# Summing the rotation's two products with accumulating transfers instead of vector adds, in a fused attention and feed-forward kernel

## The chip, the core and the metric

One core of a Trainium2 chip runs the whole program. The metric is the device time of one execution in microseconds, taken here as the median of three executions. TensorE (PE in the rows, with its weight loads shown apart as PEld), VectorE (DVE), ScalarE (ACT), GpSimd (POOL) and SyncE (SP) each work through their own list of instructions in order; transfers run on 16 DMA engines beside them.

## The reference

Four sequences, eight heads, 576 positions, 64 columns a head. Queries and keys are first rotated, then attention runs, and its output goes through two feed-forward blocks.

```python
def rotate(x):
    x1, x2 = (x[..., :half], x[..., half:])
    return np.concatenate([x1 * cos - x2 * sin, x1 * sin + x2 * cos], axis=-1)
q_rot, k_rot = (rotate(q), rotate(k))
scores = scale * np.matmul(q_rot, k_rot.transpose(0, 1, 3, 2))
attn = softmax(scores)            # minus the row's maximum, exp, over the row's sum
attn_out = np.matmul(attn, v)
...
x = x_attn.reshape(2304, 512)
x = ((x @ w1) * (x @ w2)) @ w3 @ w_out                       # first block
out = np.maximum(np.maximum(x @ u1, x @ u2), x @ u3) @ u_out # second block
```

All arrays are float32 on the host's side.

## The kernel before

Every float32 number that enters a matmul is split into a high part and a low part, which three matmuls multiply (high by high, low by high, high by low). Two heads make a pair, with their 64 columns on 128 partitions, so attention is 16 pairs, numbered p = 0 to 15.

For each pair, `prepare(p)` makes the rotated keys (e = 1) and queries (e = 0). The host lays each operand out twice, once as it is and once with its halves swapped, so the rotation is: load both copies (tile `qk`, two planes of 128 x 576; for pair 1 the tile is called `early`), multiply plane 0 by the cosine table and plane 1 by the signed sine table (line 612), and **sum the two planes into plane 0** (line 614). ScalarE then casts the sum into the high part in `st` (line 618), and a subtraction makes the low part (line 619). `st` and a small tile `z` (the last 64 positions of both heads, line 441) are what the score matmuls read. There are two `st` buffers, so the parts of pair p can only be written when the scores of pair p - 2 are done. There is one `qk` buffer for keys and one for queries.

After that, per pair: scores on TensorE (tile `s`, line 423), the row's maximum on VectorE (line 668), exp on ScalarE (line 671, tile `p`), transposes on TensorE (tile `t`, line 676), their split on ScalarE and VectorE (lines 441 and 708, tile `pt`), the product with v (tile `pv`), and the scaling by the reciprocal row sums (`inverse`, lines 681 and 683, and `rows_done`). Between these, TensorE folds two weight matrices into one (tile `m` from `wo` and `w`), and then runs the first block's two products (also tile `m`). The weights arrive as 64-bit words that VectorE and ScalarE turn into float32 (`convert`, lines 506, 509 and 511). From 458 us on no attention work is left and TensorE runs the two blocks.

**What sets the order.** Each operation is a task with an engine, a priority and a planned duration. A planner in the program walks the tasks in planned time and puts each ready task of the lowest priority next on its engine. A table of numbers, `MOVES`, perturbs the priorities, and also the engine of those tasks that can run on one of two engines (`either`). So the table fixes each engine's list, and it is a part of the program text. A transfer's task has a `tail`, the planned length of the transfer after its issue. Loads and stores are all issued by SyncE (`load`, line 444).

Of the kernel before, what the change touches and what calls it, by code (L numbers as in the profile page):

```python
# [46 lines left out]
    10000024, 10000032, 10000048, 10000067, 10000110, 10000112, 10000169, 10000173, 10000183, 10000227, 10000237,  # L47
    10000252, 10000323, 10000357, 10000392, 10000453, 10000476, 10000488, 10000538, 10000610, 10000693, 10000728,
    10000735, 10000773, 10000840, 10000846, 10000909, 10001099, 10001126, 10001173, 10001205, 10001233, 10001384,
    10001401, 10001457, 10001485, 10001511, 10001518, 10001545, 10001635, 10001784, 10001833, 10001865, 10001872,  # L50
    10001929, 10002157, 10002158, 10002193, 10002284, 10002338, 10002497, 10002607, 10002618, 10002634, 10002684,
    10002970, 10003189, 10003196, 10003281, 10003343, 10003405, 10003407, 10003435, 10003527, 10003634, 10003636,
    10003647, 10003666, 10003686, 10003773, 10004011, 10004536, 10004770, 10004918, 10004919, 10004999, 10005035,
    10005145, 10005476, 10005486, 10005506, 10005662, 10005664, 10005765, 10005914, 10006123, 10006241, 10006294,
    10006442, 10006576, 10007147, 10007203, 10007507, 10007547, 10007556, 10007604, 10007777, 10007815, 10008037,
    10008371, 10008436, 10008857, 10009245, 10009375, 10009463, 10009964, 10010205, 10010668, 10010822, 10011063,
    10011153, 10011320, 10011733, 10011754, 10012451, 10013224, 10013724, 10013750, 10013752, 10014503, 10014800,
    10015034, 10015238, 10015292, 10016008, 10016071, 10016400, 10016686, 10016975, 10016998, 10017598, 10018086,
    10018994, 10019298, 10019480, 10019796, 10019820, 10020198, 10020898, 10021153, 10021422, 10021641, 10021659,
    10022452, 10022683, 10022959, 10023141, 10023268, 10023299, 10023504, 10023897, 10024188, 10024325, 10024358,  # L60
    10024944, 10026610, 10027292, 10027429, 10027638, 10027768, 10028459, 10028793, 10030569, 10031137, 10031647,
    10031679, 10032588, 10033141, 10034705, 10034759, 10036016, 10036114, 10036487, 10037496, 10037920, 10038523,
    10038572, 10038623, 10038861, 10038948, 10039345, 10039953, 10040004, 10040208, 10041169, 10041777, 10042003,
    10042306, 10042544, 10043181, 10043748, 10043993, 10044060, 10044981, 10045250, 10046335, 10047230, 10048349,
    10050783, 10052317, 10053102, 10053375, 10053441, 10054365, 10054616, 10055368, 10055784, 10056263, 10056510,
    10058185, 10058223, 10058413, 10058664, 10060609, 10061682, 10061930, 10063544, 10063652, 10063701, 10064328,
    10064930, 10065410, 10065600, 10065736, 10065897, 10066392, 10068294, 10068310, 10069270, 10069399, 10069478,
    10070709, 10070855, 10071006, 10071578, 10071647, 10071991, 10072861, 10074691, 10075956, 10076571, 10076918,
    10077155, 10077393, 10077402, 10078340, 10079070, 10079133, 10080360, 10080621, 10081686, 10081820, 10082428,
    10083020, 10083021, 10083344, 10084928, 10085257, 10086848, 10087495, 10088943, 10089683, 10090879, 10091498,  # L70
    10091855, 10092674, 10092784, 10092916, 10093174, 10094606, 10094899, 10098752, 10101220, 10101843, 10101960,
    10102171, 10103117, 10105007, 10105660, 10107129, 10108351, 10109018, 10110088, 10113960, 10116148, 10116306,
    10116538, 10118489, 10119480, 10123241, 10124490, 10126498, 10126937, 10127867, 10128934, 10129888, 10132550,
    10134240, 10135241, 10136106, 10138483, 10139877, 10140809, 10141009, 10141359, 10141814, 10142075, 10142417,
    10142735, 10143382, 10143576, 10144461, 10145622, 10146303, 10147616, 10149250, 10149696, 10151815, 10151995,
    10153576, 10155729, 10157912, 10159162, 10159394, 10166681, 10169703, 10170189, 10171770, 10171897, 10173462,
    10176946, 10180597, 10181204, 10181835, 10182805, 10184517, 10186706, 10187211, 10188223, 10189780, 10193794,
    10194085, 10196598, 10197990, 10205021, 10205075, 10206304, 10207559, 10212827, 10213856, 10218775, 10234307,
    10235000, 10235644, 10238566, 10239970, 10266620, 10267709, 10275199, 10275926, 10279327, 10281026, 10283592,
    10287879, 10290827, 70012376, 70015660, 70026858, 70030643, 70045947, 70049814, 70051889, 70054017, 70055280,  # L80
    70056770, 70066295, 70067872, 70074298, 70078855, 70083392, 70083724, 70084529, 70086923, 70087171, 70087261,
# [1129 lines left out]
```

## Time and profile before

| | |
|---|---|
| median of three executions | 926.19 us (925.84 to 928.98) |
| profiled execution, own time | 927.38 us |
| its span, first to last instruction | 925.4 us |
| around the span | 1.98 us |
| TensorE busy | 891.0 us, 96% of the span |
| VectorE busy | 633.0 us, 68% |
| ScalarE busy | 475.9 us, 51% |
| GpSimd busy | 342.4 us, 37% |
| granted TensorE clock, mean | 0.998 of 2.4 GHz |

The profiled execution is 1.19 us above the median, so a change in the span is read against 925.4 us, and the forecast is then made on the median. A busy share is a mean over stages with different limits; the stages are read apart further down.

### The profile page before, as it was taken

Reading aid. Unit: us, or ns where it says so; the run is one execution under the profiler, and the core shown is the slowest. Engines: PE = TensorE matmul, PEld = TensorE weight load, DVE = VectorE, ACT = ScalarE, POOL = GpSimd, SP = SyncE. Lnnn points to the kernel's source line nnn. Section 1 sums busy time; section 2 is a strip of 40 time slices with the busy share of each in tenths; the row PEclk is TensorE's granted clock in tenths of the full one; section 3 lists DMA queues with packets and bytes.
Section 4 is the critical chain, followed back from the end, with each engine's and each line's share of the span. In section 5 each row is a group of like instructions: output and inputs, shape, how many; then the busy total and the mean of one; then the engine's idle time right before and its main releaser. Section 6 shows DMA issues by size and latency. Waiting matters only on the chain.

```text
span 925.4 us, 16273 instructions
## 1 busy us (share of the span) xinstructions
PE 891.0 (96%) x5922; PEld 823.8 (89%) x5922; DVE 633.0 (68%) x1133; ACT 475.9 (51%) x1054; POOL 342.4 (37%) x332
## 2 busy tenths in 40 slices
PE   1898999999999999999999999999999999999998
PEld 1666769989999999999998999999999999999886
DVE  6997988898867677687766333657988577578300
ACT  4677887876757577567544222434323322334411
POOL 3645767766436366522110000433332333232000
PEclk9999999999999999999999999999999999999999
DMA  8454546542333123310147543323324114255511
GB/s 265 134 188 153 165 154 209 149 142 84 100 103 97 44 92 93 97 50 18 37 153 213 199 127 89 103 86 97 98 86 140 55 46 148 68 163 195 201 57 68
DMA packets 80287, 110.31 MB, mean 119 GB/s; under 512 B 27984, under 2 KB 61008, under 8 KB 80208
## 3 DMA queue, kind: packets, MB, share of 16 engines
q1 hardware_dynamic: 80208, 109.29, 37.4%
q8 instruction: 46, 0.75, 0.3%
q14 instruction: 33, 0.27, 0.1%
HBM read 83.76 MB, written 25.50 MB: 118 GB/s over the span
## 4 chain that ended last, share of the span: by engine, by line
PE 80%; DVE 9%; DMA 7%; issue 2%; ACT 1%; SPq 1%; POOL 0%; DVEq 0%; ACTq 0%
PE q L423 46%; PE m L423 15%; PE t L676 7%; PE pv L423 6%; PE s L423 6%; DVE pt L708 3%; DMA raw<-in_w3t_dram 3%; DVE sm L668 2%; DMA raw<-in_w_dram 2%; DVE raw L509 1%; DMA rawc<-in_w3t_dram 1%; SPq L444 1%; DMA vr<-in_vv_dram 1%; DVE cw L511 1%; ACT pt L441 0%
## 5 line engine op out<-in xcount | busy, mean ns | idle before, releaser
L708 DVE TENSOR_TENSOR pt<-t,pt 128x320 fp32r<-128x320 f32 (+3 forms) x256 | 132.4, 528 | 34.5 <-ACT pt L441 29.4
L441 ACT CAST pt<-t 128x320 fp32r<-128x320 f32 (+3 forms) x234 | 103.5, 456 | 51.9 <-PE t L676 24.9
L423 PE MATMUL pv<-pt,v 128*128 128x256 f32 (+1 forms) x576 | 113.2, 317 | 5.1 <-DVE pt L708 4.0
L668 DVE TENSOR_REDUCE sm<-s 128x1 f32<-128x576 f32 x144 | 103.9, 749 | 19.8 <-PE s L423 18.8
L423 PE MATMUL q<-gt,wp 128*128 128x384 f32 x576 | 100.0, 334 | 0.0
L423 PEld LDWEIGHTS q<-gt,wp 128*128 128x128 f32 x576 | 99.8, 188 | 0.0
L423 PEld LDWEIGHTS pv<-pt,v 128*128 128x128 f32 x576 | 82.8, 189 | 15.7 <-DVE pt L708 9.5
L423 PE MATMUL s<-st 64*128 64x288 f32 x768 | 71.7, 316 | 18.7 <-ACT st L618 11.7
L423 PEld LDWEIGHTS s<-st 64*128 64x128 f32 x768 | 55.6, 190 | 32.5 <-ACT st L618 11.7
L423 PE MATMUL q<-yc__7620,u 128*128 128x384 f32 x378 | 71.2, 340 | 0.0
L423 PE MATMUL q<-yc__7946,u 128*128 128x384 f32 x378 | 70.8, 340 | 0.0
L423 PE MATMUL q<-yc__7376,u 128*128 128x384 f32 x378 | 70.5, 340 | 0.0
L423 PEld LDWEIGHTS q<-yc__7946,u 128*128 128x128 f32 x378 | 67.1, 188 | 0.1
L423 PEld LDWEIGHTS q<-yc__7620,u 128*128 128x128 f32 x378 | 67.1, 188 | 0.0
L423 PEld LDWEIGHTS q<-yc__7376,u 128*128 128x128 f32 x378 | 67.1, 188 | 0.0
L441 ACT COPY tmp<-q 128x384 f32<-128x384 f32 x45 | 21.5, 479 | 84.7 <-PE q L423 84.5
L441 ACT COPY ga<-q 128x512 f32<-128x512 f32 (+2 forms) x34 | 16.9, 497 | 65.6 <-PE q L423 61.6
L1066 POOL TENSOR_TENSOR tmp<-tmp 128x384 f32<-128x384 f32 x20 | 22.6, 1132 | 72.3 <-ACT tmp L441 72.3
L423 PE MATMUL q<-tail,tail 128*128 128x512 f32 x216 | 49.1, 389 | 0.0
L423 PEld LDWEIGHTS q<-tail,tail 128*128 128x128 f32 x216 | 40.5, 188 | 8.4
L522 DVE TENSOR_TENSOR gt<-gt 128x768 fp32r<-128x768 f32 x24 | 26.7, 1117 | 25.3 <-ACT gt L521 25.3
L1079 DVE TENSOR_TENSOR tmp<-q,tmp 128x384 f32<-128x384 f32 x54 | 29.9, 554 | 15.4 <-PE q L423 15.2
(1222 smaller groups left out, 2050.9 us busy)
## 6 DMA issues: line engine op xcount, KB each, us to landing
gt<-g_d SPq DMA_DIRECT2D x24, 384.0 KB
raw<-in_m_dram SPq DMA_DIRECT2D x72, 128.0 KB
raw<-in_w_dram SPq DMA_DIRECT2D x16, 512.0 KB
h_d<-top SPq DMA_DIRECT2D x36, 192.0 KB
tail<-h_d SPq DMA_DIRECT2D x36, 192.0 KB
raw<-in_wo_dram SPq DMA_DIRECT2D x12, 512.0 KB
raw<-in_w3t_dram SPq DMA_DIRECT2D x12, 512.0 KB
g_d<-ga SPq DMA_DIRECT2D x32, 160.0 KB
```

The lines of the kernel that those rows point to most:

```text
L423: pe.matmul(o, a, b, start=start, stop=stop, **kw)
L441: (e.copy if e is act else e.tensor_copy)(o, i)
L444: return add("SP", .5, lambda: sync.dma_start(o(), src()), r, w, part, deps, prio, tail=us)
L509: add("DVE", 0.42, lambda: dve.tensor_scalar(low_word(), low_word(), 29, None, ALU.logical_shift_right), part=[raw], deps=raw.writers, pri ...
L511: add("DVE", 0.69, lambda: dve.scalar_tensor_tensor(u(), u(), 3, low_word(), ALU.logical_shift_left, ALU.bitwise_or), r=[raw], deps=[first ...
L522: either(sb(n, "DVE"), lambda on: on.tensor_tensor(sel()[:, LO], f32(sel()[:, LO]), f32(sel()[:, HI]), ALU.subtract), r=[dst], part=[dst], ...
L668: add("DVE", c_dve(S), lambda s=s, col=col: dve.tensor_reduce(sm.t[:, 0, col:col + 1], s.t[:, :, :288], axis=AX.XY, op=ALU.max, negate=Tru ...
L676: pe.transpose(o, x, ident.t)
L708: add("DVE", c_dve(n), lambda: dve.tensor_tensor(low(pt.t), src(t.t), f32(hi(pt.t)), ALU.subtract), r=[t], part=[pt], deps=[h], prio=prio)
L1066: either(sb(TN), lambda on: on.tensor_tensor(s5.t, s1.t, s5.t, ALU.add), r=[s1], w=[s5], prio=prio)
L1079: add("DVE", c_dve(TN), lambda: dve.tensor_tensor(e.t, at_(o), e.t, ALU.add), r=[accs[o]], w=[e], prio=prio)
```

## The change

From pair 1 on, the add of line 614 is no longer an instruction of GpSimd or VectorE. GpSimd issues a transfer that reads plane 1 of the tile from SBUF and accumulates it into plane 0. Pair 0 keeps its adds. The table that orders the work is a new one.

```diff
 MOVES = (
-    10000024, 10000032, 10000048, 10000067, 10000110, 10000112, 10000169, 10000173, 10000183, 10000227, 10000237,
...
+    30000054, 30000057, 30000069, 30000081, 30000085, 30000090, 30000130, 30000134, 30000136, 30000311, 30000359,
...
 )
...
-            k = either(sb(S, first), lambda on, t=t: on.tensor_tensor(t.t[:, 0], t.t[:, 0], t.t[:, 1], ALU.add),
-                       part=[t], deps=last, prio=prio)
+            if p == 0:
+                k = either(sb(S, first), lambda on, t=t: on.tensor_tensor(t.t[:, 0], t.t[:, 0], t.t[:, 1], ALU.add),
+                           part=[t], deps=last, prio=prio)
+            else:
+                k = add("POOL", 1.0, lambda t=t: pool.dma_start(t.t[:, 0], t.t[:, 1], accum_op=ALU.add),
+                        part=[t], deps=last, prio=prio, tail=1.2, lock=False)
```

The new program is nine lines shorter above the edit and five below it, so its line 603 is the old 612, 606 the old 611 and 614 (the add of pair 0), 609 the new transfer, 613 the old 618, 614 the old 619, 634 the old 639, 435 the old 444.

What moves at the start, on SyncE, the queue of the loads: in both programs pair 0's first products need a table and a plane of `qk`. Before, `qk0__113` holds the queries and comes first, and `qk1__118` the keys:

```order
L444 DMA tabs0__107<-in_cs_dram 128x576
L444 DMA tabs1__111<-in_cs_dram 128x576
L444 DMA qk0__113<-in_qk_dram 128x576 x2
L444 DMA vr_116<-in_vv_dram 128x5x64
L444 DMA qk1__118<-in_qk_dram 128x576 x2
L444 DMA vr_116<-in_vv_dram 64x5x64
```

and of the change, where `qk1__115` holds the keys and `qk0__124` the queries:

```order
L435 DMA tabs1__107<-in_cs_dram 128x576
L435 DMA ident_111<-in_cs_dram 128x128
L435 DMA vr_113<-in_vv_dram 128x5x64
L435 DMA qk1__115<-in_qk_dram 128x576 x2
L435 DMA vr_113<-in_vv_dram 64x4x64
L435 DMA tabs0__119<-in_cs_dram 128x576
L435 DMA vr_113<-in_vv_dram 64x5x64
L435 DMA qk0__124<-in_qk_dram 128x576
L435 DMA vr_113<-in_vv_dram 64x64
L435 DMA qk0__124<-in_qk_dram 128x576
```

The last of the four planes was the sixth load and is now the eleventh, behind the identity matrix and all of `vr` (the values).

On VectorE the same stretch, before and then of the change (`v` and `vr` are the values' split, `st` the high and low parts):

```order
L612 TENSOR_TENSOR qk1__118<-qk1__118,tabs0__107 128x576
L612 TENSOR_TENSOR qk1__118<-qk1__118,tabs1__111 128x576
L614 TENSOR_TENSOR qk1__118<-qk1__118 128x576
L639 TENSOR_TENSOR v_143<-vr_116,v_143 128x10x64
L619 TENSOR_TENSOR st_147<-qk1__118,st_147 128x576
```

```order
L603 TENSOR_TENSOR qk0__124<-qk0__124,tabs2__137 128x576
L603 TENSOR_TENSOR qk0__124<-qk0__124,tabs3__122 128x576
L634 TENSOR_TENSOR v_141<-vr_113,v_141 128x10x64
L606 TENSOR_TENSOR qk0__124<-qk0__124 128x576
L614 TENSOR_TENSOR st_144<-qk1__115,st_144 128x576
```

The split of the values now stands ahead of the second sum of pair 0 instead of behind it.

On GpSimd, from the two clearings of `z` on, before and then of the change (`early` is pair 1, the next `qk` pair 2; ISA is the instruction that configures GpSimd's code):

```order
L614 ISA
L614 TENSOR_TENSOR early_126<-early_126 128x576
L614 TENSOR_TENSOR early_130<-early_130 128x576
L612 TENSOR_TENSOR qk0__174<-qk0__174,tabs2__122 128x576
L619 TENSOR_TENSOR st_211<-early_130,st_211 128x576
L619 TENSOR_TENSOR st_211<-early_126,st_211 128x576
```

```order
L432 CAST z0__105<-st_144 64x2x64
L609 DMA early_128<-early_128 128x576
L603 ISA
L603 TENSOR_TENSOR qk1__157<-qk1__157,tabs0__119 128x576
L609 DMA early_130<-early_130 128x576
L603 TENSOR_TENSOR qk0__178<-qk0__178,tabs2__137 128x576
L603 TENSOR_TENSOR qk0__178<-qk0__178,tabs3__122 128x576
L614 TENSOR_TENSOR st_214<-early_128,st_214 128x576
L614 TENSOR_TENSOR st_214<-early_130,st_214 128x576
```

The second transfer of pair 1 stands behind a product of pair 2, and the configuring instruction behind the first transfer.

## Rows read from the trace of the kernel before

**Rows 1.** Page of the profile: span, and TensorE's busy time in us.
```profile
span 925.4 us, 16273 instructions
...
PE 891.0 (96%) x5922; PEld 823.8 (89%) x5922; DVE 633.0 (68%) x1133; ACT 475.9 (51%) x1054; POOL 342.4 (37%) x332
```

**Rows 2.** Busy time of each engine by stage: stretch, its length, busy us.
```profile
0.00:38.20 38.20, 16.68 (x103) 13.29 (x104) 28.20 (x43) 20.16 (x41) 16.56 (x16) 1.00 0.59 185
38.20:67.30 29.10, 26.11 (x155) 18.58 (x155) 26.38 (x50) 22.46 (x53) 14.45 (x13) 0.94 0.60 202
67.30:185.90 118.60, 113.70 (x808) 92.06 (x809) 102.04 (x181) 96.44 (x229) 83.14 (x69) 1.00 0.55 170
185.90:458.30 272.40, 271.33 (x2228) 254.29 (x2225) 205.97 (x399) 180.43 (x454) 128.68 (x118) 1.00 0.26 80
458.30:921.40 463.10, 462.82 (x2634) 445.61 (x2633) 270.41 (x463) 155.80 (x277) 99.54 (x117) 1.00 0.37 119
```

**Rows 3.** TensorE's waits in the first 120 us: us, times, longest.
```profile
PE s L423 <- ACT st L618: 11.7, 1, 11.7
PE s L423 <- ACT p__187 L671: 5.4, 2, 4.3
```

**Rows 4.** Timeline of the start: start us, duration us, engine, line, tiles.
```profile
0.74 0.39 SPq L444 DMA_DIRECT2D tabs__107<-in_cs_dram  x1
...
3.60 0.68 ACT L609 ACTIVATE tabs__122<-tabs__107 128x576 f32<-128x576 f32 x1 [1.58 <-DMA tabs__107<-in_cs_dram]
...
5.50 0.76 DVE L612 TENSOR_TENSOR qk__113<-qk__113,tabs__122 128x576 f32<-128x576 f32 x1 [5.50 <-DMA qk__113<-in_qk_dram]
...
8.79 0.76 DVE L612 TENSOR_TENSOR qk__118<-qk__118,tabs__111 128x576 f32<-128x576 f32 x1 [0.21 <-DMA qk__118<-in_qk_dram]
...
10.48 0.83 DVE L639 TENSOR_TENSOR v<-vr,v 128x640 fp32r<-128x640 f32 x1
10.95 0.67 ACT L618 CAST st<-qk__113 128x576 fp32r<-128x576 f32 x1
...
11.67 0.61 PE L423 MATMUL s<-st 64*128 64x288 f32 x2 [11.67 <-ACT st L618]
...
17.15 1.40 POOL L614 TENSOR_TENSOR early<-early 128x576 f32<-128x576 f32 x1 [0.81 <-DVE early L612]
17.18 1.66 DVE L509 TENSOR_SCALAR raw<-raw 128x512 uint32<-128x512 uint32 x1
...
20.05 1.57 POOL L612 TENSOR_TENSOR qk__174<-qk__174,tabs__122 128x576 f32<-128x576 f32 x1 [1.50 <-DMA qk__174<-in_qk_dram]
...
24.93 0.19 ACT L671 ACTIVATION_READ_ACCUMULATOR p__219<-s,sm 128x1 f32 x1
```

**Rows 5.** Line 614, the sums: duration ns min/median/max, first and last start.
```profile
L614 POOLq MODIFY_POOL_CONFIG  x2: 11/11/11, 1.2 to 1.3; - x2
L614 POOL TENSOR_TENSOR early<-early x2: 1402/1712/2022, 14.3 to 17.1; 128x576 f32<-128x576 f32 x2
...
L614 POOL TENSOR_TENSOR qk__1796<-qk__1796 x1: 1403/1403/1403, 168.2 to 168.2; 128x576 f32<-128x576 f32 x1
```

**Rows 6.** Busy time of line 614 alone, 11.6 to 185.9 us.
```profile
sum 174.30, DVE 0.75 POOL 20.82; mean DVE 0.12 POOL 3.47
```

**Rows 7.** Line 618, the cast that reads the sum.
```profile
L618 ACT CAST st<-qk__1796 x1: 672/672/672, 175.5 to 175.5; 128x576 fp32r<-128x576 f32 x1
```

**Rows 8.** Line 509, VectorE's shift in the weights' conversion, two views.
```profile
L509 DVE TENSOR_SCALAR raw<-raw x34: 408/440/1659, 17.2 to 492.4; 128x512 uint32<-128x512 uint32 x34
...
L509 DVE TENSOR_SCALAR raw<-raw 128x512 uint32<-128x512 uint32 x34 | 26.2, 773 | 8.6 <-DMA raw<-in_w3t_dram 5.2 <-DMA raw<-in_w_dram 3.1
```

**Rows 9.** Chain that ended last: a load on the path, start, us.
```profile
181.68 6.41 DMA raw<-in_w_dram
```

**Rows 10.** Timeline of VectorE, two low parts of line 619.
```profile
38.62 0.76 DVE L619 TENSOR_TENSOR st<-qk__174,st 128x576 fp32r<-128x576 f32 x1
...
62.42 1.33 DVE L619 TENSOR_TENSOR st<-qk__416,st 128x576 fp32r<-128x576 f32 x1
```

83 rows, old and new, of the table MOVES are left out of this document.

## The prediction

> **What bounds the kernel now.** I read the page's busy line first, then the stages, then who TensorE waits for, then the start in order of time. TensorE is busy 891.0 of 925.4 us [rows 1], so at most 34.4 us of idle time can be won. The stages say where it lies [rows 2]: 21.5 us before 38.2 us, 3.0 us in the next 29.1, 4.9 us up to 185.9 us, then 1.1 us in 272.4 and 0.3 us in 463.1. From 186 us on TensorE is the bound and GpSimd is busy less than half the time, so there a cheaper sum on GpSimd buys nothing as long as it is in time. What the change can be worth lies before 186 us. In that stretch VectorE is the busiest engine beside TensorE (26.38 of 29.1 us, then 102.04 of 118.6), and the largest waits of TensorE are for the first cast of pair 0, 11.7 us, and for the first exponentials, 5.4 us [rows 3]. The start is thus a chain: loads, rotation, cast, scores, maximum, exp. Each later microsecond on it is paid.
>
> **Term 1, the head of the chain: +1.0 us.** VectorE's fifth instruction waits for the fourth plane of pair 0 and starts at 8.79 us; its first waited for the first plane until 5.50 us [rows 4]. Ahead of the first landing stand 864 KB (two tables and a plane of 288 KB each), ahead of the other 1888 KB (two tables, four planes, 160 KB of values). That is 1024 KB in 3.29 us, 311 KB a us. In the new list the last plane comes after both tables, four planes, 64 KB of identity and 320 KB of values: 2112 KB, so 0.7 us later, at 9.5 us. That product (0.76 us), then the split of the values (0.83), now ahead, then the sum (0.76, as the product) end at 11.9 to 12.0 us; the cast's 0.67 us follows, and the first score starts near 12.7 instead of 11.67 us [rows 4]. Nothing hides this; I carry +1.0 us to the exponentials.
>
> **Term 2, the transfers' latency: 0, with up to 3 us if it is long.** No row shows GpSimd issuing a transfer or one that accumulates. Its length from issue to use is bounded from below by the load of a table with the same 288 KB: issued at 0.74, used at 3.60 us, so 2.9 us [rows 4]. From above I take the longest load on the path, 6.41 us for 512 KB among others [rows 9]. I take 4.0 us: it is as big as the table's, but reads its destination too, and pair 1's runs beside loads. The time of GpSimd itself lies between SyncE's 0.39 us for such an issue [rows 4] and 2.02 us, the longest sum of `early` [rows 5]; I take 1.0 us, inside the 4.0.
>
> Where is a late sum seen? For pairs 3 to 15 the cast that reads it waits for its `st` buffer. The shortest such distance belongs to the tile whose sum runs from 168.2 to 169.6 us and whose cast starts at 175.5 [rows 5, 7]: 7.3 us after the sum's start. So 4.0 us, and 6.4 us too, are hidden by the wait for pair p - 2's scores. If that cover went, ScalarE would stand at the cast, with the split of the probabilities queued behind it and TensorE behind that.
>
> Pair 1 has no such cover. Behind the sum that ends at 12.0 us VectorE has five instructions of 0.76 us up to both products of the first transfer, which is thus issued near 15.8 and lands near 19.8 us. The second is queued on GpSimd behind a product of pair 2 that waits for its load, which before landed at 20.05 us; that product takes 1.57 us [rows 4]. So it is issued at 21.6 and lands at 25.6 us. ScalarE comes to that cast right behind the exponentials that ended at 25.1 us [rows 4], now 26.1; to the first one two exponentials earlier, so that it has the time too. The second is hidden by 0.5 us at 4.0, and 1.9 us late at 6.4. Behind the transfer on GpSimd stand two products of pair 2 and pair 1's low parts, which pair 1's scores don't read until after 36 us in the old order; they have the slack.
>
> **Term 3, VectorE's work in the second stage: -1.4 us.** Between the first and second reciprocal of line 683, which bound the second stage of rows 2 to within half a microsecond, VectorE ran one sum of pair 3 (0.75 us, the one instance of line 614 in rows 6 that is VectorE's) and two low parts, 0.76 and 1.33 us [rows 10]. The new list has none of the three in that stretch: 2.84 us less on an engine that is 91% busy there [rows 2]. Idle TensorE time in the stage is 3.0 us, so not all can come through; I take half, 1.4, with ends at 0 and 2.8. What other rows of the new order gain or lose between 67 and 186 us I can't read from a list; I put it at 0, with 2.5 us either way, about half the 4.9 us of idle there.
>
> **Term 4, less crowding of VectorE by GpSimd: -0.3 us.** VectorE's shift of line 509 takes 408 ns at best, 1659 at worst, in the mean 773 against a median of 440 [rows 8], so 34 of them lose 11.3 us. The worst starts at 17.18 us while GpSimd's sum of 17.15 runs for 1.40 us [rows 4]: the one waits out the other. Up to 185.9 us GpSimd is busy 114.2 us [rows 2], 20.8 of it with sums [rows 6]. Fourteen issues of 1.0 us in their place leave 6.8 us, 6%, less, so 0.7 us of the 11.3; half of it on the path is 0.3. At 0.39 us an issue it would be 0.8, at 2.02 us a loss of 0.4.
>
> A rule speaks against this term. The Trainium skill, "SBUF — State Buffer", section "Who interferes with whom", says that a transfer issued by GpSimd needs GpSimd's port to write its descriptors, and that VectorE in a two-port mode locks it out for the whole instruction. The row on line 509 shows that lock for arithmetic; no run here shows it for an issue. By the rule the issues would take part in the same exclusion and the relief would be nearer 0, the sum -0.4 instead of -0.7 us.
>
> **The sum.** +1.0 + 0 - 1.4 - 0.3 = -0.7 us. Against the profiled execution that is 927.38 - 0.7 (its span 925.4 - 0.7); against the median, which lies 1.19 us lower, 926.19 - 0.7 = 925.5 us. About 0.5%, 4.6 us, is what a measurement of this kernel can tell from no change.
>
> **Rivals.**
>
> *The order wins back the start's idle time (17%).* For it: 7.9 us of TensorE idle time between 38.2 and 186 us, and VectorE's relief there. If all of term 3 (2.8), the 2.5 us of the unread moves and the 0.8 of term 4 come through without term 1's loss, it is 6.1 us: 920 us. Against it: the lists are alike in their heads, and term 1 is a visible loss.
>
> *The transfers land late (9%, slower).* The place is ScalarE, standing at pair 1's second cast and then pair 2's two. It decides from 4.5 us issue to landing on. At 6.4 us the first costs 1.9 us; two more such stands make 5.7, and with term 1, and no relief, 6.7 us: 932.9 us. For it: the start's DMA engines are 0.59 busy [rows 2]. Against: the table's 2.9 us.
>
> *GpSimd's code configuration is exposed (6%).* The instruction that configures GpSimd ran at 1.2 us, 13 us ahead of the first vector instruction at 14.3 us [rows 5], so any time that it costs was hidden. Now it stands behind the first transfer, near 17 us, and the product behind it can start at 20.05 at the earliest [rows 4]: 3 us stay hidden. By rows its cost is anything from 0 to 13 us, the exposed part 0 to 10, all of it on pair 1's second sum, of which 0.5 us is slack: 925.5 to 935 us. Halfway, 5 us exposed, it is 930. The Trainium skill, "GPSIMD Engine Reference", section "Instruction dispatch", puts the first call after a load of code at about 6 us, unseen in the profile; by that figure 3 us would be exposed and the time 928. No row of before tells.
>
> *My forecast, a change too small to tell, with the mechanisms above: 68%.* All low ends at once (+1.0 - 2.8 - 2.5 - 0.8) would be 921.1 us, all high ones (+1.0 + 1.9 + 2.5 + 0.4) 932.0; they are unlikely to meet, and some two thirds of the way to each, 922.5 to 930 us, is its own range.
>
> **The numbers.** Faster by over 0.5% (under 921.6): 0.18, the first rival and a tail of the forecast. Slower by over 0.5% (over 930.8): 0.13, the late landing and half of the code's. The rest, 0.69. For 8 in 10 the range reaches into both sides: 919.5 to 931.5 us.
>
> **What would show it.** Right: the first score near 12.7 us; the transfers 3 to 5 us from issue to landing, and no wait of ScalarE's casts for a transfer after pair 2; GpSimd busy about 1 us an issue; TensorE's idle time after 186 us unchanged near 1.5 us. Wrong: a wait of ScalarE for `early`'s or `qk`'s transfer in the first 40 us, a gap of GpSimd behind the configuring instruction, or TensorE waiting for `st` in the middle of the attention.

## The result: 1.35% slower

The changed kernel took 939.22 us in the median against 926.02 us for the kernel before, a ratio of 1.0135 with a 95% interval of 1.0102 to 1.0169. The prediction had 925.5 us. Its four executions lay in two pairs, at 937.5 and at 941 us. The profiled one has a span of 935.6 us, 10.2 us more than the 925.4 us of before.

The page of the changed kernel, busy line and the new queue (packets, MB, share of 16 engines):

```profile
PE 893.7 (96%) x5922; PEld 824.2 (88%) x5922; DVE 639.2 (68%) x1152; ACT 468.4 (50%) x1033; POOL 340.2 (36%) x334
...
q0 software_dynamic: 4320, 8.85, 5.4%
```

TensorE's busy time rose by 2.7 us [rows 1], so most of the 10.2 us is idle time. The stages of the changed kernel, and two short stretches at the end (columns as in [rows 2]):

```profile
0.00:38.20 38.20, 14.58 (x82) 11.79 (x82) 24.41 (x33) 16.45 (x32) 15.27 (x19) 0.96 0.73 209
38.20:67.30 29.10, 26.13 (x165) 18.59 (x164) 27.53 (x50) 23.94 (x58) 17.96 (x16) 1.00 0.76 207
67.30:185.90 118.60, 109.30 (x750) 86.33 (x749) 101.44 (x180) 91.14 (x218) 72.46 (x64) 0.99 0.64 183
32.70:36.10 3.40, 3.35 (x15) 2.81 (x13) 2.77 (x5) 1.90 (x5) 3.40 (x4) 0.50 0.85 218
145.40:148.70 3.30, 3.30 (x19) 2.97 (x20) 2.12 (x5) 2.63 (x6) 1.99 (x2) 0.50 0.53 162
```

Against [rows 2] TensorE is busy 2.1 us less in the first 38.2 us, the same in the second of these stretches, and 4.4 us less from 67 to 186 us. In the two short stretches its clock was granted at 0.50, the 1.2 GHz level; both follow a delay that is told of below. A matmul of `pv` (128x256) takes 415 ns in the first of them and 282 ns in the median at 1.0, so TensorE's busy time grows there. Before, one such stretch of 3.4 us stood at 38.3 us. The waits of TensorE (us in total, times, longest):

```profile
PE s L414 <- ACT st L613: 14.5, 1, 14.5
PE t L671 <- DVE pt L703: 5.5, 5, 1.4
PE pv L414 <- DVE pt L703: 5.4, 6, 1.8
PE s L414 <- ACT p__189 L666: 4.5, 1, 4.5
```

The wait for the first cast is 2.8 us longer than in [rows 3], and waits for VectorE's splits of the probabilities (line 703) make 10.9 us, where before had 5.7 (its line 708). The start, rows of several engines, from 23 us on GpSimd's first and then the others' (line 609 is the new transfer, 500 and 502 VectorE's operations on words, 663 the maximum, 666 the exponential):

```profile
6.60 0.59 SPq L435 DMA_DIRECT2D qk__124<-in_qk_dram  x1
...
11.55 0.76 DVE L603 TENSOR_TENSOR qk__124<-qk__124,tabs__122 128x576 f32<-128x576 f32 x1 [0.72 <-DMA qk__124<-in_qk_dram]
12.23 0.82 DVE L634 TENSOR_TENSOR v<-vr,v 128x640 fp32r<-128x640 f32 x1
...
14.47 0.61 PE L414 MATMUL s<-st 64*128 64x288 f32 x2 [14.47 <-ACT st L613]
...
23.14 0.88 POOL L609 DMA_DIRECT2D early<-early  x1
23.75 1.71 POOL L603 TENSOR_TENSOR qk__178<-qk__178,tabs__137 128x576 f32<-128x576 f32 x1
25.11 1.70 POOL L603 TENSOR_TENSOR qk__178<-qk__178,tabs__122 128x576 f32<-128x576 f32 x1
26.47 1.71 POOL L614 TENSOR_TENSOR st<-early,st 128x576 fp32r<-128x576 f32 x1
...
24.86 3.62 DVE L500 TENSOR_SCALAR raw<-raw 128x512 uint32<-128x512 uint32 x1
28.39 0.74 DVE L663 TENSOR_REDUCE sm<-s 128x1 f32<-128x576 f32 x1
29.06 0.41 DVE L500 TENSOR_SCALAR raw<-raw 128x512 uint32<-128x512 uint32 x1
...
29.17 0.74 ACT L666 ACTIVATE p__218<-s,sm 128x576 f32<-128x576 f32 x1 [3.37 <-DVE sm L663]
```

Two things are to be seen. The last plane of pair 0 is issued at 6.60 us and used at 11.55, and the first score comes at 14.47 instead of 11.67 us [rows 4]. And at 24.86 us a shift of words, 0.42 us when nothing hinders it, takes 3.62 us: it ends as the third of three GpSimd instructions behind the issue at 23.14 ends. The next maximum, and ScalarE's exponential, wait for it. Up to 200 us four operations on words took over 1.9 us (3.62, 2.75, 2.43 and 2.94 us at 24.86, 79.08, 106.27 and 141.55), each in a run of GpSimd instructions behind an issue. Before, none did; the longest shift was 1.66 us [rows 8]. Below, "long operations" are those of over 1.9 us on words before 200 us.

### The profile page after: what moved, and what is told of

Its sections match the earlier page's. It is cut to its first block, busy times and chain, and to the rows that moved or that the text cites. A ratio compares the mean times of both kernels' runs of the same rounds, so it can differ in the third digit from the quotient of the medians.

```text
span 935.6 us, 16335 instructions
## 1 busy us (share of the span) xinstructions
PE 893.7 (96%) x5922; PEld 824.2 (88%) x5922; DVE 639.2 (68%) x1152; ACT 468.4 (50%) x1033; POOL 340.2 (36%) x334
## 4 chain that ended last, share of the span: by engine, by line
PE 83%; DVE 7%; DMA 4%; ACT 3%; issue 2%; SPq 1%; POOL 0%; ACTq 0%; DVEq 0%; POOLq 0%
PE q L414 48%; PE m L414 15%; PE t L671 7%; PE pv L414 6%; PE s L414 6%; DVE pt L703 2%; DVE sm L663 2%; ACT pt L432 1%; DMA raw<-in_w3t_dram 1%; DVE raw L500 1%; SPq L435 1%; DMA raw<-in_w_dram 1%; DMA vr<-in_vv_dram 1%; DMA qk__124<-in_qk_dram 1%; DMA r_d<-rt 0%
## 5 line engine op out<-in xcount | busy, mean ns | idle before, releaser
L414 PE MATMUL pv<-pt,v 128*128 128x256 f32 (+1 forms) x576 | 115.4, 319 | 6.8 <-DVE pt L703 5.4
L663 DVE TENSOR_REDUCE sm<-s 128x1 f32<-128x576 f32 x144 | 104.3, 751 | 19.9 <-PE s L414 18.8
L414 PEld LDWEIGHTS pv<-pt,v 128*128 128x128 f32 x576 | 83.6, 191 | 18.2 <-DVE pt L703 10.9
L432 ACT COPY tmp<-q 128x384 f32<-128x384 f32 x40 | 19.2, 480 | 96.3 <-PE q L414 89.2
L513 DVE TENSOR_TENSOR gt<-gt 128x768 fp32r<-128x768 f32 x23 | 24.6, 1071 | 36.3 <-ACT gt L512 35.2
L512 ACT CAST gt<-gt 128x768 fp32r<-128x768 f32 x24 | 20.1, 836 | 41.3 <-DMA gt<-g_d 41.2
L1061 POOL TENSOR_TENSOR tmp<-tmp 128x384 f32<-128x384 f32 x19 | 20.6, 1086 | 47.7 <-ACT tmp L432 37.8
```

What stands on the lines that cost most here:

```text
L414: pe.matmul(o, a, b, start=start, stop=stop, **kw)
L432: (e.copy if e is act else e.tensor_copy)(o, i)
L512: add("ACT", c_act(n), lambda: act.copy(sel()[:, HI], f32(sel()[:, LO])), r=[dst], part=[dst], prio=prio)
L513: either(sb(n, "DVE"), lambda on: on.tensor_tensor(sel()[:, LO], f32(sel()[:, LO]), f32(sel()[:, HI]), ALU.subtract), r=[dst], part=[dst], ...
L663: add("DVE", c_dve(S), lambda s=s, col=col: dve.tensor_reduce(sm.t[:, 0, col:col + 1], s.t[:, :, :288], axis=AX.XY, op=ALU.max, negate=Tru ...
L1061: either(sb(TN), lambda on: on.tensor_tensor(s5.t, s1.t, s5.t, ALU.add), r=[s1], w=[s5], prio=prio)
```

## Experiments

### List and sum taken apart

Each expectation names its own theories; the letters hold within a group. The first run keeps the new list and undoes the transfers; the second puts transfers into the old list; the third and fourth drop the table of numbers from both kernels (`MOVES = ()`).

```
e1, on the changed kernel; e2 does the reverse on the kernel before, for its 29 sums on GpSimd
-  lambda t=t: pool.dma_start(t.t[:, 0], t.t[:, 1], accum_op=ALU.add)
+  lambda t=t: pool.tensor_tensor(t.t[:, 0], t.t[:, 0], t.t[:, 1], ALU.add)
```

> The changed kernel's list of work, row for row on every engine, but each of the 30 sums from the second pair on is GpSimd's own addition again (about 1.4 us each) and no transfer. Theory A (the order found by the new search costs the time, the form of the sum little): the time stays by the changed kernel's 939 us, 935 to 945. Theory B (the transfers cost it: their landing, or GpSimd's issuing of them): the time falls back by most of the 13 us, to 926 to 931.

> The list of the kernel before, row for row on every engine, with the 29 sums that GpSimd made there emitted as accumulating transfers (the one on VectorE stays). Theory A: within 3 us of the kernel before, 924 to 929. Theory B: slower by 8 to 13 us, 934 to 939. A third reading, that transfers gain where the order is good because GpSimd is relieved by some 0.5 us a sum: 921 to 924.

> The kernel before without its table of numbers, so that the planner's first list is issued. With the next run it shows what the change does where neither list was searched. Both theories: slower than 926, by an amount that no trace shows yet (an estimate, from nothing but the some 10 us of idle TensorE time before the span's first 40 us: 10 to 40 us).

> The changed kernel without its table of numbers. Theory A: within 5 us of the run without the table and with additions, on either side, since the form of the sum is worth little and the lists differ. Theory B: slower than that run by 8 us or more.

Measured: the new list with additions 931.21 us (ratio 1.0047, 1.0028 to 1.0066); the old list with transfers 928.37 (1.0020, 1.0004 to 1.0036); without tables 956.65 with additions (1.0333, 1.0300 to 1.0366) and 956.79 with transfers (1.0339, 1.0293 to 1.0385). The first is just outside B's range, the second inside A's; neither theory holds alone. By the ratios the list costs 0.47%, 4.4 us, and in it the transfers another 0.88%, 8.1 us; in the old list the transfers cost 1.9 us, and without the tables the two kernels are equal. There were no long operations in e1, e2 and e3, four in e4, where they cost nothing that shows (its list differs from e3's too). In e2 ScalarE's first cast of `early` waited 3.9 us for its transfer, the longest wait for a landing there. The same shift in e1, in the order of time, still has a GpSimd instruction beside it and waits for that one alone:

```profile
24.36 1.34 DVE L500 TENSOR_SCALAR raw<-raw 128x512 uint32<-128x512 uint32 x1
```

### Issue, bytes, words and head, one at a time

```
e5, on e1: a small accumulating transfer behind each addition
+  pool.dma_start(t.t[:, 1, 0:1], t.t[:, 0, 0:1], accum_op=ALU.add)
e6, on e1: a transfer of 576 KB at the same place, issued by SyncE, that nothing waits for
+  sync.dma_start(x_d[p][e], qk[p][:, 2 * e:2 * e + 2])
e7, on the changed kernel: VectorE's nth operation put behind another
+  for n, behind in ((17, 20), (19, 17), (99, 102), (142, 146), (143, 142), (200, 204), (202, 200)):
+      seq.remove(dve[n])
+      seq.insert(seq.index(dve[behind]) + 1, dve[n])
e8, on the changed kernel: SyncE's first eleven loads in another order
+  for i, n in zip(at, (0, 6, 3, 4, 2, 8, 10, 5, 7, 9, 1)):
+      seq[i] = head[n]
```

> The changed kernel's list with additions (931.2 us by the earlier run), and behind each of the 30 additions GpSimd issues an accumulating transfer of one element a row into the plane that is dead by then. So it has GpSimd's 30 issues and nearly none of the transfers' bytes, and no sum waits for one. Theory A (behind an issue GpSimd's instructions overlap, each starting some 0.3 us before the one ahead has ended, and VectorE's operations on words, lines 500 and 502, stay shut out for the whole run of them): 935 to 940 us, with at least one such operation of over 1.9 us, up to 3 or 4, before 190 us. Theory B (the 288 KB of each transfer crowd the loads, or land late): 931 to 934 us and no such operation over 1.9 us.

> The changed kernel's list with additions, and at the place of each SyncE issues a transfer of 576 KB from memory to memory that nothing waits for: more time on the DMA engines than an accumulating transfer takes (1.7 us of all 16 each, from the share of 5.4% over 30), and no issue by GpSimd. It leaves the results as they are. Theory A: 931 to 934 us, no operation of lines 500 and 502 over 1.9 us. Theory B: 936 to 942 us, with longer waits for loads of raw and qk.

> The changed kernel, transfers and all; only the four operations on words that took 2.4 to 3.6 us in its trace (at 24.86, 79.08, 106.27 and 141.55 us), with those of their own that must follow, stand behind the two or three maxima and splits that waited behind them. Theory A: these maxima and splits come 2 to 3 us earlier at each place, and some of it reaches the end: 931 to 936 us. Theory B: the lists differ by nothing that counts there, 937 to 941.

> The changed kernel with one thing altered: its first eleven loads stand in the order of the kernel before (both tables and the first tile's planes, 160 KB of values, the second tile's planes, then the rest of the values and the identity). Theory of the head (the first score came 2.8 us late because the last plane is SyncE's eleventh issue instead of its seventh, at 6.60 us instead of about 3.85): first score at 11.7 to 12.2 us and 936 to 937 us. Rival (the start's DMA engines are the limit, by bytes, 0.7 us): first score at 13.5 to 14 us and 938.5 us.

Measured: 958.93 us for the issues alone (1.0358, 1.0318 to 1.0398), 933.77 for the bytes alone (1.0086, 1.0071 to 1.0101), 946.05 with the words later (1.0208, 1.0165 to 1.0250), 935.92 with the loads reordered (1.0108, 1.0059 to 1.0158). The issues without their bytes cost some 28 us over e1, three times what theory A allowed, with long operations of 7.45, 5.07, 4.15 and 5.58 us. The crowding costs some 2.6 us, within theory A's 931 to 934: e6's loads and its added transfers hold all 16 DMA engines 52 us longer than e1's, about as long as the accumulating transfers do (5.4% of 935.6 us, 51 us), and it has no long operation.

e7 went the wrong way by both theories. Its first shift was put behind a maximum that itself waited 3.4 us for scores, and was then shut out behind the next issue (2.35 us); near 84 us ScalarE began to wait 4.1 us for a load into `raw`, whose buffer the postponed operation had kept. It tells nothing on the price of the shut-out.

e8 shows where the head's delay came from. Its VectorE in order of time:

```profile
9.74 0.75 DVE L603 TENSOR_TENSOR qk__118<-qk__118,tabs__122 128x576 f32<-128x576 f32 x1
11.33 0.83 DVE L634 TENSOR_TENSOR v<-vr,v 128x640 fp32r<-128x640 f32 x1 [0.85 <-ACT v L633]
12.08 0.75 DVE L606 TENSOR_TENSOR qk__118<-qk__118 128x576 f32<-128x576 f32 x1
```

The last plane is now there when it is wanted, 1.8 us sooner; but the split of the values stands ahead of pair 0's second sum and waits, so that the first score comes at 13.59 us, which is the rival's figure, not at 11.7 to 12.2. Loads and split share the 2.8 us.

### The cost by itself, and the head undone

```
e9: one of its stretches, 18 in all
  sync.dma_start(gate, cs[:, 0:S]); act.copy(late, gate); act.copy(late, late)
  times(pool, runs[4], gate)
  pool.dma_start(pair[0][:, 0], pair[0][:, 1], accum_op=ALU.add)
  for n in range(4): times(pool, runs[n], runs[n])
  times(dve, mine, late)
  for t in word: shift(t)
e10, on e1: loads as in e8, and
+  for e, n, behind in (("ACT", 2, 4), ("DVE", 5, 9)):
+      own = [k for k in seq if k.eng == e]
+      seq.remove(own[n])
+      seq.insert(seq.index(own[behind]) + 1, own[n])
...
```

> The disputed cost by itself; none of the reference's work is done and the output is zeros. Three times over, six stretches of the same five GpSimd multiplications (128x576, 1.40 us each when alone) with two of VectorE's shifts of words (128x512, 0.42 us each when alone) let loose beside them some 2 us in: with no transfer; with an accumulating transfer of 288 KB issued by GpSimd behind the first multiplication; with a plain one; with an accumulating one of one element a row; with the large one and GpSimd's next multiplication held back until some 4 us after the first; and with the large one and VectorE's multiplications of 576 in the place of the shifts. Theory A (an issue lets GpSimd's following instructions overlap by 0.3 us, and a shift stays out for the whole run): shifts wait for at most one instruction, 0.4 to 1.7 us, with no transfer, and 3 to 6 us with each of the three kinds; with GpSimd held back, as without one. Rival (the transfer's bytes or its adding do it): the small or the plain one leaves the shifts under 1.7 us. Second rival (the long waits are chance): no difference between the stretches.

> The changed kernel's list with additions (931.2 us), with the first eleven loads in the order of the kernel before, and the first cast and split of the values behind pair 0's own casts and low parts. If the head's loss is loads and values' split together: first score at 11.6 to 12.2 us, and 928 to 929 us, so that with the transfers undone as well 2 to 3 us of the 13 are left to the rest of the list. If the loads alone are it, the first score comes no sooner than in the run with only the loads changed, 13.6 us, and the time is near 930 us.

e9, GpSimd and VectorE in order of time (two shifts to a row); the stretches are no issue, a large accumulating one, a large plain copy, GpSimd held back:

```profile
18.21 5.95 POOL L64 TENSOR_TENSOR run<-run 128x576 f32<-128x576 f32 x4
18.89 2.66 DVE L67 TENSOR_SCALAR word<-word 128x512 uint32<-128x512 uint32 x2
...
29.89 1.00 POOL L76 DMA_DIRECT2D pair<-pair  x1
30.63 4.74 POOL L64 TENSOR_TENSOR run<-run 128x576 f32<-128x576 f32 x4
30.58 6.77 DVE L67 TENSOR_SCALAR word<-word 128x512 uint32<-128x512 uint32 x2
...
43.04 2.68 DVE L67 TENSOR_SCALAR word<-word 128x512 uint32<-128x512 uint32 x2
...
69.13 2.91 DVE L67 TENSOR_SCALAR word<-word 128x512 uint32<-128x512 uint32 x2
```

With no issue the shifts slip in between GpSimd's instructions, 1.37 us each. Behind the accumulating issue the first takes 6.43 us, until all five are through, and the second takes 0.42. One element a row does the same (6.64 us for the two), so it is not the bytes; with GpSimd held back it is gone. VectorE's multiplications with both inputs in SBUF are shut out as well (7.28 us for two in two rounds; in the third the one ahead of them took 6.97). The plain copy did nothing here, in all three rounds, which looked like the accumulating kind being the cause; e17 and e18 show that it is not.

e10 took 931.07 us (1.0049, 1.0035 to 1.0063), e1 931.21. Its first score came 2.9 us sooner than e1's:

```profile
11.80 0.61 PE L414 MATMUL s<-st 64*128 64x288 f32 x2 [11.80 <-ACT st L613]
```

By 40 us 0.6 us of it was left, at the end nothing. In its profiled execution the granted clock stood at 0.50 from 34.3 to 41.1 us, where e1's stayed at 1.0, and this took a part of the gain; but executions with a mean clock of 1.0 show no gain either (spans of 926.8 to 930.5 us, e1's of 926.9 and 927.4). The head is not what the list lost; the expected 928 to 929 us was wrong.

### Holding GpSimd behind the issue

```
e11, on the changed kernel, at four of the transfers; e12 at all 30
+  pool.memset(t.t[:, 1, 0:1], 0.0)     # behind the issue, waits for its landing
```

> The changed kernel, transfers and all, with one thing added at four of the 30 transfers (those behind which the four long operations on words stand in its trace): GpSimd clears one dead element a row behind the issue, which has to wait for the transfer's landing, some 3.5 us. By the run of the cost by itself GpSimd's instructions then no longer overlap. Theory A: no operation of lines 500 and 502 over 1.9 us at these places, the maxima and splits behind them 1 to 2.5 us sooner, and 932 to 936 us; GpSimd had 2 to 9 us of idle time behind three of the four, which pays for the hold. Rival (the transfers cost by landing late and crowding, not by shutting VectorE out): 939 to 942 us, since a hold only makes GpSimd later.

> The same hold behind all 30 transfers, so that GpSimd never overlaps behind one; it stands idle some 2.7 us more at each, 36 us over the first 190 us where it was busy 116. Theory A: no operation on words over 1.9 us anywhere, and, as GpSimd's lateness takes part of it back, 933 to 938 us. Rival: 941 us or more.

e11 took 940.95 us (1.0155, 1.0130 to 1.0181), which is what the rival said. All four long operations were gone, but two others had come, 2.43 us at 34.74 and 3.04 us at 138.19, each behind an issue without a hold. In place of the first, ScalarE stood at pair 1's first cast, whose transfer was issued at 17.10 us and landed 8.7 us later:

```profile
25.83 0.67 ACT L613 CAST st<-early 128x576 fp32r<-128x576 f32 x1 [5.13 <-DMA early<-early]
```

TensorE stood 4.8 us for the exponential behind that cast. So in the start the late landing seems to lie in parallel to the shut-out, and taking one away shows the other. e12 took 978.15 us with no long operation, on the rival's side (941 or more). Its granted clock stood at 0.95 even in the second half, where TensorE hardly waits:

```profile
400.00:960.00 560.00, 556.80 (x3414) 533.83 (x3413) 347.68 (x623) 214.37 (x427) 138.92 (x150) 0.95 0.36 109
```

Why stays open, but it is not what made the kernel slower: a matmul of `q` from `gt` and `wp` takes 334 ns in that half, as it does in the changed kernel at 1.0. TensorE is idle for 65.2 us in e12 against 41.8, and its clock stood at 0.50 for 30.6 us before 411 us against 6.8. A hold behind every transfer thus costs more than the shut-outs that it removes.

### Which transfers, and which part of them

```
e13, on e1: the small accumulating issue of e5 at four places only
e14, on the changed kernel: additions at these four places
e15, on the changed kernel: additions for p < 7
e16: the changed kernel again
e17, on e13: the four as plain copies
+  at in ((1, 0), (4, 1), (5, 0), (6, 1)) and pool.dma_start(t.t[:, 1, 0:1], t.t[:, 0, 0:1])
```

> The changed kernel's list with additions (931.2 us) and GpSimd's issue of an accumulating transfer of one element a row at four places alone, those behind which the changed kernel's long operations on words stand. No sum waits for a transfer, and next to no bytes move. Theory A (the shut-out is most of the 8 us): at least two operations of lines 500 and 502 over 1.9 us there, and 934 to 939 us. Theory L (landing late and crowding are most of it): 930 to 933 us.

> The changed kernel with GpSimd's additions at these four places, and transfers at the other 26. Theory A: 932 to 935 us. Theory L (all 14 transfers of the first 190 us share the loss): 936 to 939 us.

> The changed kernel with additions for pairs 1 to 6 and transfers from pair 7 on, all of them issued after 160 us. If the transfers' loss lies in the first 160 us, as the traces have it: 930 to 933 us. If transfers cost wherever they stand: 935 us or more.

> The changed kernel again, on the same chip as the three runs above, since its earlier runs lay at 937.5 and at 941 with nothing between: 937 to 941 us.

> The run with four issues (949.4 us), the same four small transfers at the same places, but plain copies instead of accumulating ones. If it is the accumulating issue that shuts VectorE out, as in the run of the cost by itself: no operation on words over 1.9 us, and 930 to 934 us. If four small transfers or their waits cost of themselves, whatever their kind: 940 us or more.

Measured: 949.36 us for four issues (1.0234, 1.0209 to 1.0259), beyond theory A's 939; 936.62 with four sums (1.0101, 1.0081 to 1.0121), 930.88 with only late transfers (1.0041, 1.0024 to 1.0059), 942.78 for the changed kernel again (1.0156, 1.0121 to 1.0191), above the expected 937 to 941; 948.47 for four plain copies (1.0238, 1.0213 to 1.0263). All of the transfers' loss lies with pairs 1 to 6, since with the 18 from pair 7 on alone the time is e1's. Four issues of next to no bytes cost some 17 us in the list with additions, where GpSimd's runs behind them are longer. VectorE in order of time in e13, then TensorE behind its three long operations (the third of 4.55 us at 148.68):

```profile
24.72 8.53 DVE L500 TENSOR_SCALAR raw<-raw 128x512 uint32<-128x512 uint32 x1
33.17 0.74 DVE L663 TENSOR_REDUCE sm<-s 128x1 f32<-128x576 f32 x1
...
83.00 5.08 DVE L502 SCALAR_TENSOR_TENSOR w<-w,raw 128x512 uint32<-128x512 uint32 x1
...
34.83 0.61 PE L414 MATMUL s<-st 64*128 64x288 f32 x2 [6.00 <-ACT p__249 L666]
88.53 0.48 PE L671 MATMUL t<-ident,p__542 128*128 128x128 f32 x1 [3.41 <-DVE pt L703]
153.73 0.58 PE L414 MATMUL pv<-pt,v 128*128 128x256 f32 x1 [3.40 <-DVE pt L703]
```

So each long operation is followed by a pause of TensorE, 12.8 us in all; from 22 to 200 us e1 has none over 1.6 us. During the second and third the granted clock fell to 0.50, for 6.8 us each. Of the 18.8 us by which the span is longer than e1's, TensorE is idle for 11.1 and busy for 7.6.

e16's profiled execution, with a span of 944.0 us, shows how the changed kernel can come out slower from the same list. In VectorE's list two maxima have a shift between them and one behind them:

```profile
23.73 0.48 DVE L500 TENSOR_SCALAR raw<-raw 128x512 uint32<-128x512 uint32 x1
24.14 0.74 DVE L663 TENSOR_REDUCE sm<-s 128x1 f32<-128x576 f32 x1
24.80 8.03 DVE L500 TENSOR_SCALAR raw<-raw 128x512 uint32<-128x512 uint32 x1
```

The shift that took 3.62 us above came 0.14 us ahead of the issue here and took 0.48; the next one, which took 0.41 us above, was caught. Above, the shut-out held up a maximum, an exponential and pair 1's second cast, for which GpSimd then waited 2.46 us, and the run ended after three instructions; here the cast came in time and the run went on for 8 us. ScalarE's first cast of `early` also waited 4.0 us for its transfer instead of 1.6, and the clock stood at 0.50 for 13.6 us instead of 6.8. These are two executions; how the other ones divide was not seen.

Four sums in the place of transfers took 936.62 us, which is in theory L's range (936 to 939) and not in A's. They gained 6.2 us over e16 on the same chip and 2.6 over the first measurement. One long operation of 5.53 us stayed at 131 us, behind another issue, and TensorE stood 5.67 us behind it; so the four places were not all of the shut-outs.

e17 was expected at 930 to 934 us if the accumulating kind were the cause. It is not: plain copies cost as much, with long operations of 8.21, 4.77 and 4.16 us. The last run separated what is left.

```
e18: a stretch of e9, varied in kind, size, what the issue reads, and the shifts' moment
  times(pool, p[:, 1] if after else runs[4], gate)
  if kind: pool.dma_start(p[:, 0, 0:n], p[:, 1, 0:n], **({"accum_op": ALU.add} if kind == "sum" else {}))
  ...
  dve.tensor_reduce(red, late, axis=AX.X, op=ALU.max)
  for t in word: shift(t)
```

> The cost by itself again; none of the reference's work is done and the output is zeros. Each stretch: a GpSimd multiplication, an issue, five more GpSimd multiplications; beside them two of VectorE's shifts of words, let loose by ScalarE behind two, three or four of its copies of 0.7 us. The issue is left out, or a plain copy or an accumulating transfer, of one element a row or of 288 KB, and it reads either a tile that was long done or the one that the multiplication ahead has just written. Two rounds of all 27. Readings: (1) an accumulating issue alone shuts the shifts out: all 24 of its stretches show a shift of 2.5 us or more, and none of the plain ones; (2) an issue of any kind does where it follows GpSimd's own result: both kinds with the tile just written, neither without; (3) a small plain copy does as an accumulating one does, and only the large plain copy does not, whatever it reads; (4) the moment at which the shift comes decides: the three delays differ more than the kinds. In each the stretches with no issue show shifts of at most 1.7 us.

Every issue does it here, so the first three readings fall; the moment changes how long the wait is, by 1.4 us, and the kind by 0.3, but neither decides whether there is one. In all 48 stretches with one, whatever its kind, size or source, the first shift stayed out until GpSimd's run was through, 4.6 to 6.7 us by its moment; in the six without one no shift took over 1.37 us. No issue, then the small and the large plain copy, in order of time:

```profile
18.62 2.05 DVE L67 TENSOR_SCALAR word<-word 128x512 uint32<-128x512 uint32 x2
...
29.63 6.51 DVE L67 TENSOR_SCALAR word<-word 128x512 uint32<-128x512 uint32 x2
...
54.37 6.34 DVE L67 TENSOR_SCALAR word<-word 128x512 uint32<-128x512 uint32 x2
```

Theory A of e5 and e9 took the cause to be that GpSimd's instructions overlap behind an issue. They do so by some 0.3 us behind the accumulating ones, but behind the 24 plain ones each starts within 0.07 us of the end of the one ahead, as it does without an issue, and the shift stays out all the same. So the overlap isn't the cause, and why an issue does it stays open.

In e9's plain stretches VectorE's own multiplication was still running (42.37 to 43.13 us) when GpSimd's run began at 42.97; here its instruction ahead is a maximum with one input. That may be why those three came out otherwise, and wasn't varied.

## Why the prediction was wrong

**Term 4, less crowding of VectorE by GpSimd: the step that failed.** I priced an issue as so much less GpSimd time (-0.3, ends -0.8 and +0.4), as if VectorE's wait were in proportion to it. What it changes is whom the wait is for: one GpSimd instruction without an issue, the whole run behind one. e1, e5, e13 and e18 show this, and in the new list the transfers lose 8.1 us in the place of a gain of 0.3. That most of the 8.1 is the shut-out is argued, not measured: crowding alone costs some 2.6 us in e6, a landing that keeps a cast waiting 3.9 us goes with 1.9 us in the old list (e2), and e11 shows that the landing can take the shut-out's place. The sum also has no term for TensorE's clock. In the profiled executions the changed kernel's span is 6.2 us longer than e1's, and 2.5 us of that is TensorE's busy time, with 6.8 us at 0.50, where e1's clock stayed at 1.0 from 30 to 928 us.

The Trainium skill, "SBUF — State Buffer", section "Who interferes with whom", says that whoever issues first has the shared ports for the whole instruction. The stretches without an issue agree (1.37 us for a shift beside instructions of 1.32); behind an issue it is 6.43 us and five instructions, and there the measurement decides. The prediction took from that section only that the relief would be nearer 0.

**Term 1, +1.0: mis-sized at its place, and wrong at the end.** The first score came 2.8 us later. I ordered the landings by bytes, which gave 0.7 us for the last plane; it stood as SyncE's eleventh issue, at 6.60 us, and with the loads in the old order it was issued 2.6 us and used 1.8 us sooner (e8). "Nothing hides this" was wrong too: e10 undid all of it and ended where e1 did.

**Term 2, 0: the middle was right, the place was not free.** The transfers' line shows issue to landing of:

```profile
DMA to landing us min/median/max: 3.4/4.1/6.6
```

I had taken 4.0, and 1.0 us an issue (0.84 to 1.23 measured). The longest one, pair 1's first, kept ScalarE's cast waiting 1.6 us, the one wait for such a transfer in this execution; the prediction had named a wait for `early` as a sign of being wrong. So the rival of late landing was seen, one cast earlier than it said and with that wait instead of 5.7 us (4.4 us, in two casts, in e16).

**Term 3, -1.4: smaller, and outweighed.** The prediction bounded the second stage by the first two reciprocals. They stood at 37.92 and 67.06 us before and at 41.83 and 68.30 us now, so its fixed edges would compare different work. Between the reciprocals, before and then of the change (columns as in [rows 2]):

```profile
37.92:67.06 29.14, 26.12 (x155) 18.59 (x155) 26.39 (x49) 22.46 (x53) 14.45 (x13) 0.94 0.61 202
41.83:68.30 26.47, 24.35 (x148) 16.85 (x148) 24.93 (x46) 21.99 (x53) 17.96 (x16) 1.00 0.79 221
```

VectorE is busy 1.5 us less, not 2.84, and TensorE is idle for 2.1 us instead of 3.0, so 0.9 us came through. The stretch is shorter by another 1.8 us of TensorE's busy time, with seven matmuls fewer and at a clock of 1.0, where before had its 3.4 us at 0.50.

The prediction put the unread moves at 0, with 2.5 us either way; they cost instead. In e1, the new list with additions, TensorE is idle 2.5 us longer than before up to 40 us and 3.2 us less from there to 96. Behind that the list's loss shows in two stretches; the kernel before, then e1 (columns as in [rows 2]):

```profile
96.00:135.00 39.00, 37.01 (x240) 27.04 (x239) 33.39 (x61) 32.30 (x80) 28.88 (x23) 1.00 0.50 152
280.00:480.00 200.00, 199.45 (x1628) 188.17 (x1626) 143.12 (x285) 127.25 (x318) 80.96 (x77) 1.00 0.22 69
```

```profile
96.00:135.00 39.00, 34.74 (x231) 25.45 (x230) 35.50 (x63) 30.70 (x75) 27.05 (x23) 1.00 0.51 166
280.00:480.00 200.00, 197.58 (x1605) 184.91 (x1605) 145.08 (x292) 124.35 (x311) 77.52 (x72) 1.00 0.21 64
```

TensorE idles 2.3 us more in the first, where VectorE has 2.1 us more to do, and 1.9 more in the second: 4.1 us together, where the list costs 4.4. The second lies behind the 186 us up to which the prediction looked. Which moves they are was not tried.

**The other rivals.** The order won nothing back by itself. The code configuration was not exposed: the instruction that configures GpSimd ran at 18.25 us, and the one behind it started at 21.46 as its load landed. The Trainium skill, "GPSIMD Engine Reference", section "Instruction dispatch", has some 6 us for a first call; only 3.2 us lie between the two rows, so by that figure 2.8 would have been exposed, and none is seen.

## What to carry to other kernels

Before a transfer is moved to GpSimd, look at what GpSimd runs behind the issue: VectorE's shifts, and its multiplications of two tiles in SBUF, waited behind an issue for that whole run, in all stretches but e9's three plain ones. So the issue belongs where GpSimd waits next anyway, or, where the kind of transfer allows it, to another engine (e6, issued by SyncE, had no long operation); a wait put in for the purpose gained nothing here (e11) or cost more (e12). Then follow TensorE: what counts is whether an operation that it needs stands behind the one shut out. Judge a cheaper instruction in a searched list by undoing it in that same list, since the list and the instruction can each lose on their own. Order a start's loads by the issuing queue's time, some 0.4 to 0.7 us an issue, as well as by bytes.

## What the runs showed of the hardware

- A transfer issued by GpSimd, plain or accumulating, of 512 bytes or 288 KB in all, shuts VectorE's shifts out of the run of GpSimd instructions behind it: 48 of 48 stretches in e18, 4.6 to 6.7 us against at most 1.37 us without an issue. In e9 the six stretches with an accumulating one right ahead of GpSimd's run show it too, the three with a plain one do not. Where GpSimd waited in between, the shift took 1.62 us.
- A multiplication of VectorE with both inputs in SBUF is shut out too (7.28 us for two).
- GpSimd's instructions overlap by some 0.3 us behind an accumulating issue and not behind a plain one (e18); the shut-out comes with both.
- Which operation of VectorE is caught can change from one execution to the next: a shift of 3.62 us and the next of 0.41 in the one with a span of 935.6 us, 0.48 and 8.03 us in the one with 944.0.
- An accumulating transfer of 288 KB takes 3.4 to 6.6 us to land in the changed kernel, 4.1 in the median; the first one of the start took 6.6, and 7.5 and 8.7 in e16 and e11.
- A granted clock of 0.95 in e12 left a matmul at the 334 ns that it takes at 1.0; at 0.50 a `pv` matmul takes 415 ns instead of 282.
